# Two transformer layers on one core: W1 and W3 copied once into a layout by units, one load per unit, and a new order of the work

## The chip, the cores and the metric

One Trainium2 chip, of which the kernel uses one core. The metric is the time of one execution on the device in microseconds (us); lower is better. The kernel before took 2657.01 us in the median of three runs (2655.47 to 2658.84).

## What is computed

The input x has 2048 rows of 576 numbers (bf16). Two layers follow one another, with the same weights; each is an attention with a recurrent memory and then a gated feed-forward network (FFN). Cut to what matters:

```
def _A_ref(x, mem0, Wq, Wk, Wv, Wo, seg_len):      # 32 heads of 128, 8 memory rows, seg_len 32
    mem = mem0
    for s in range(n_seg):                          # 64 segments, one after the other
        h = concatenate([mem, x[:, s*32:(s+1)*32]]) # 40 rows
        q, k, v = h Wq, h Wk, h Wv
        p = softmax(where(mask, q k^T * 128**-0.5, -1e9))
        o = (p v) Wo
        mem = o[:, :8]                              # the next segment needs it
        outs.append(o[:, 8:])
def _B_ref(x, w1, w3, w2):                          # w1, w3: 576 x 4608, w2: 4608 x 576
    return (silu(x w1) * (x w3)) w2
for _ in range(2):
    x = x + _A_ref(layernorm(x), ...)
    x = x + _B_ref(layernorm(x), ...)
```

## The kernel before

**Steps.** The 64 segments of a layer form a chain through mem. The second layer runs eight segments (LAG) behind the first, so there are 72 steps; step t works on segment t of layer 0 and on segment t - 8 of layer 1. Steps 8 to 63 have both ("both", 80 columns per matmul), the first and the last eight have one layer (40 columns). After every four steps a job of FFN work becomes possible (128 rows of each layer).

**Pieces.** `make_nodes` (from line 248) cuts the work into nodes: an engine, a duration in us that the planner books, what they need, a priority, and the buffers they take and give back. On TensorE each kind has a letter (line 90): Q and q are the projections to q and k (512 rows of the contraction, and the last 64 rows as "tail"), S the scores, T a transpose of the softmax weights on TensorE (steps with one layer only), P the weighted sum, O and o the output projection and its tail, V, v, X, x, G, g the projections to v, F and f a unit of x w1 and x w3, W and w the products with w2 of two units, n, a, b the transposes behind a layernorm, p that of the attention's output, m that of mem0.

**Order.** `plan` (line 94) lays the nodes out in time. TensorE's sequence is written out by hand, as three strings of letters (lines 217 to 238): `ORDER = FIRST + FOUR * 11 + LAST`; FOUR is four steps. The other engines take, in the planner's time, the node that can start first. Evictions may go to ACT or DVE ("AD"). What the planner then emits is a fixed order per engine; the hardware waits on semaphores where a piece isn't ready.

**Modes.** TensorE can be used as a whole, in two column halves, or in row halves or finer. A node names its modes ("full/col"). The planner keeps the mode as long as the next node allows it, and books `SWITCHES` (line 38, 0.092 to 0.098 us) for a change.

**FFN weights.** A unit is 256 columns of w1 and w3 (18 units, NPR). `load_w13` (line 761) brings a unit with four DMAs issued by SP, two of 256 KB and two of 32 KB, into one of two buffers of the tile W13; the trace names them `W<-in_B_w_dram`. A row of a unit is 512 bytes in DRAM. `load_w2` brings 256 rows of w2 (288 KB, `W2C<-in_B_w_dram`). Both are read again for each of the 17 jobs that load them; the last job takes most of its weights from W and WV (`tail_load`), whose attention weights are dead by then.

**SP's queue.** SP issues, in one order: the attention weights, the unit loads, the loads of x for the layernorm (XN), and in steps with both layers the transposes of the softmax weights as DMAs (`ptr_dma`, line 1103, `PTS<-PB`). PTS has one buffer, so a transpose can only be issued when P has read the one before. POOL issues the loads of x for the residual (XR) and the stores, and clears PB after each transpose.

**Other tiles.** OT (four slots of 640 columns) takes the evicted results of P for O; YO holds the odd half of the last output tail until the memory columns and YTS are written; YTS collects a layer's outputs for p.

Every instruction is recorded by a helper: L659 are the matmuls, L662 ACT, L665 DVE, L668 SP's DMAs, L671 ACT's DMAs, L674 POOL's DMAs.

Of the kernel before, what the change touches and what calls it, by code (L numbers as in the profile page):

```python
# [13 lines left out]
P = 128  # L14
# [19 lines left out]
PTR = 112  # L34

# [6 lines left out]
POOLS = {"bank": 8, "qkt": 4, "sme": 2, "pb": 2, "pts": 1, "ot": 4,  # L42
         "xr": 3, "xn": 2, "w13": 2, "w2": 2, "htt": 4}
# [26 lines left out]
class Node:  # L70
    __slots__ = ("eng", "dur", "fn", "deps", "prio", "mode", "acq", "rel", "name", "lat", "outs", "left", "ready",
                 "start", "end", "by", "inst")

    def __init__(self, eng, dur, fn, deps=(), prio=0.0, mode=None, acq=(), rel=(), name="", lat=None):
        self.eng, self.dur, self.fn, self.prio, self.mode = eng, dur, fn, prio, mode.split("/") if mode else mode
        self.deps = [d for d in deps if d is not None]
# [13 lines left out]
KINDS = {"m0tr": "m", "L0tr": "a", "L1tr": "b", "POST": "p", "Ftr": "n", "QK": "Q", "QKt": "q", "SC": "S", "TR": "T", "PV": "P",  # L90
# [3 lines left out]
def plan(nodes, pools, letters):  # L94
# [17 lines left out]
    order = []  # L112

# [23 lines left out]
    while len(order) < len(nodes):  # L137
# [34 lines left out]
        t_eng[e] = n.end  # L172
        for s in n.acq:
# [38 lines left out]
def ewh(*ns):  # L212
# [5 lines left out]
    "maQqSQQvqqVSxXTqSPQSTOPXoTPOTPoOoOoQqqQvSSqVqQSQTPSTOPOToPToxPOOooQqqQSqvSaVQQSqTPSTPOOoTPoTPOOooQqqQSQSvqVQTSqX"  # L218
    "SPTPOTOPoToxPOOooQqqpQvSSVqnQfFSTFfqQPWSTOPFTOfPFTofoPOOooWQFfqqfFSQQSqqfFvVfTFSPQWTSFPXffOTFPOTOPWOooooaxQqqQSW"
    "FSQvfqTVfSFPQFTfqOPSWTOPFOTffoooPFOoWQqqvSQQSFfqVfSTWqFQFSPTfPOTWPoTOPOOooobQpvVqqqQQSnQqfxFSXqqfFQQQPSWFqqfQOfS"  # L220
# [6 lines left out]
    "QqqqqQppQQvVSSnnQFfqqQFqSfQQPFfqOwPoSWFffOPFWOowoPFOoFffqqQQQQqqWSwFSGgfqqQQQPQqqgWSSGFPFffggGGPwOFOPOOffooowoFv"  # L227
    "VqqqQQQWSFqfqqQQQSwWFPSFfqqfQQPwOSWFFPoffOOWPwOoooFfqqQQWaSqqQQQbSQqgqGSQPQqqgGSOPoGggOPGwOPooOo"
# [4 lines left out]
    "QPFSTOPofFTOPwTWPOOoooFfqfqQQSQSFvqfVfqFTQPSWwSTFPxXffTFPOOTWOPwOFooooFqffqQQSWwVvqfSQFfqTQPSWTwPOSFOTfFPwTOPWOo"  # L233
    "oooFqfqfFQQWSfqSFwvVQQTSqffPWwSTFFPOoTOWPoTwPOOoobQpqxqvVSnQXqfFSQTQSPFfqOoTSFfPTwPOOoofTFPFOowQfqqQSQSFvqfVTqfF"
    "PQTSwPSXffFTOOPwTOPFOooooFxqfQQqqSvVSQTQSFPfqfOTSPwoOTFPFTOPoofOowQQfqqFSSvVqQQSqTwPTSPOOFTofPTPOOooopfffFFFnwfw"
    "FFffFFwfFffFwffwFFFFffwFwfffFFFwffFFwfffFFww"
# [11 lines left out]
def make_nodes(em, nseg, pools, o=Opt, dma_bw=230e3, load_bw=345e3):  # L248
# [24 lines left out]
    def load(name, nbytes, prio, fn, deps=()):  # L273
        return node("DMA", nbytes / load_bw, fn, deps=deps, prio=prio, name=name, lat=2.0)

    ld_m0 = node("ACT", 0.1, em.load_m0(), prio=-90, name="m0", lat=2.5)
    ld_t = [load("ldt", kb(3 * R64, 4096), -10.0, em.load_tails(0)), node("ACT", 0.1, em.load_tails(1), prio=-120, name="ldt", lat=6.0)]
    node("ACT", 0.1, em.load_tails(2), prio=-80, name="ldt", lat=6.0)
# [3 lines left out]

    b = banks(1)
# [10 lines left out]
    def ln_nodes(tag, src, xn, deps, prio, writes, warm=False):  # L294
# [5 lines left out]
        d = node("PE", 5 * 0.056, em.ln_tr(xn, b, warm), deps=[c], prio=prio, mode="col", acq=[b], rel=[xn], name=tag + "tr")  # L300
# [24 lines left out]
    vx_ev, last_v, pvs = {}, [], {}  # L325

    def v_nodes(name, t, k, prio, tail_at, emit, strips, deps, tail_deps, free):
# [3 lines left out]
        m_ = node("PE", 8 * 0.2158 + 0.11, emit(b, False), deps=deps, prio=prio, mode=modes[0], acq=b, name=name)  # L331
        n = node("PE", 0.2158, emit(b, True), deps=deps + tail_deps, prio=prio + tail_at, mode=modes[1], acq=b, name=name + "t")
# [39 lines left out]
    def step(t):  # L372
# [6 lines left out]
        mm80 = max(c80 / 2.4 + 2.5, 25.0) / 1000  # L379
        rd = reads_ht.setdefault(t, [])  # L380

# [9 lines left out]
        for g, (h0, nh) in enumerate(GROUPS):  # L391
            qs, qe = [], []
            for uh, un in units(g, nl):
# [3 lines left out]
                m_ = node("PE", 8 * un * mm80, em.qk(t, uh, un, b), deps=hx + hm[:1] + ([ld_h[g]] if t == 0 else []),  # L397
                          prio=pq, mode="full", acq=[q] + b, name="QK")
                n = node("PE", un * mm80, em.qk_tail(t, uh, un, b), deps=hx + hm + ([ld_h[g]] if t == 0 else []), prio=pq + o.qkt, mode="row",
# [3 lines left out]
                for r in (0, 1):  # L403
                    cost = ew(un * 64, un * 16) if e == 0 else ew(un * 48, un * 32)
                    qe.append(node("AD", cost if nl == 2 else ew(un * 40), em.qk_ev(t, un, r, q, b[r]), deps=[m_, n], prio=t + o.ustep * uh / 4,
                                   rel=[b[r]], name="QKe"))
# [5 lines left out]
            sc = node("PE", nh * (0.0165 * nl if nl == 2 else 0.0255), em.scores(t, g, qs, s), deps=qe, prio=pf + o.sc, mode="col" if nl == 2 else "full/col",  # L412
# [5 lines left out]
            d = node("DVE", dve(w40) + 0.2, em.sm_sum(t, g, sme), deps=[c], prio=pf, name="sum")  # L418
            w = 0.168 * (4 - e if nl == 2 else 2) + nl * w40 / 960
# [18 lines left out]
            ot = Slot("ot")  # L438
# [998 lines left out]
```

## Time and profile before

| | us |
|---|---|
| median of three runs | 2657.01 |
| the profiled execution | 2657.81 |
| its span, first to last instruction | 2656.0 |
| TensorE (PE) busy in it | 2578.3 |
| DVE busy | 2004.1 |
| ACT busy | 1242.3 |
| POOL busy | 335.2 |

The granted TensorE clock is 0.992 of full speed in the mean. A busy PE is a PE with a matmul in flight; PEld are its weight loads, which run beside it. "idle before <-releaser" tells how long an engine stood idle before an instruction and whose end let it go; "issue" means that nothing in the profile explains the wait. The times of the timeline are us from the start of the span: start, length, engine, line, operation, result and operands, count.

### The profile page before, as it was taken

Reading aid. Unit: us, or ns where it says so; the run is one execution under the profiler, and the core shown is the slowest. Engines: PE = TensorE matmul, PEld = TensorE weight load, DVE = VectorE, ACT = ScalarE, POOL = GpSimd, SP = SyncE. Lnnn points to the kernel's source line nnn. Section 1 sums busy time; section 2 is a strip of 40 time slices with the busy share of each in tenths; the row PEclk is TensorE's granted clock in tenths of the full one; section 3 lists DMA queues with packets and bytes.
Section 4 is the critical chain, followed back from the end, with each engine's and each line's share of the span. In section 5 each row is a group of like instructions: output and inputs, shape, how many; then the busy total and the mean of one; then the engine's idle time right before and its main releaser. Section 6 shows DMA issues by size and latency. Waiting matters only on the chain.

```text
span 2656.0 us, 133410 instructions
## 1 busy us (share of the span) xinstructions
PE 2578.3 (97%) x59426; PEld 2216.6 (83%) x59426; DVE 2004.1 (75%) x5137; ACT 1242.3 (47%) x3495; POOL 335.2 (13%) x399
## 2 busy tenths in 40 slices
PE   6899999999999999999999999999999999999998
PEld 4788878888888888888888888888888888888887
DVE  4677777877787778778777877877787787777866
ACT  2555453444545444454544544454444445454443
POOL 1111111110101111010101101110110111011110
PEclk8899999999999999999999999999999999999999
DMA  9055746556554655555465555645565554554458
GB/s 322 4 153 150 182 101 152 128 131 157 117 141 108 152 135 126 155 128 139 109 143 134 138 146 125 146 106 151 122 147 139 132 140 106 129 139 131 130 155 244
DMA packets 690433, 371.48 MB, mean 140 GB/s; under 512 B 234328, under 2 KB 682592, under 8 KB 689216
## 3 DMA queue, kind: packets, MB, share of 16 engines
q1 hardware_dynamic: 686320, 355.08, 53.5%
q8 instruction: 464, 7.60, 1.2%
q0 software_dynamic: 3024, 6.93, 0.9%
q10 hardware_dynamic: 512, 0.94, 0.2%
q14 instruction: 113, 0.93, 0.1%
HBM read 306.72 MB, written 2.36 MB: 116 GB/s over the span
## 4 chain that ended last, share of the span: by engine, by line
PE 83%; DMA 9%; DVE 5%; ACT 1%; issue 1%; SPq 1%; POOL 0%; ACTq 0%; DVEq 0%; POOLq 0%
PE bank L659 83%; DMA PTS<-PB 5%; DMA W<-in_B_w_dram 1%; DMA W2C<-in_B_w_dram 1%; DVE STAT L665 1%; DMA WV<-in_A_Wv_dram 1%; DVE SME L665 1%; DVE PB L665 1%; SPq L668 1%; DVE V L665 0%; DMA W<-in_A_Wq_dram 0%; ACT V L662 0%; DVE XR L665 0%; DVE HTT L665 0%; DVE LNS L665 0%
## 5 line engine op out<-in xcount | busy, mean ns | idle before, releaser
L659 PEld LDWEIGHTS <-W 128*128 128x128 bf16 (+2 forms) x32464 | 1259.9, 100 | 118.1 <-issue 63.6
L659 PE MATMUL bank<-HT,W 128*128 128x80 bf16 (+3 forms) x23040 | 785.1, 197 | 16.1 <-issue 9.3
L659 PE MATMUL bank<-XTB,W 128*64 128x256 bf16 (+5 forms) x9424 | 658.9, 263 | 2.0 <-DMA W<-in_B_w_dram 2.0
L1093 POOL MEMSET PB<- 128x1024 bf16 x288 | 273.9, 951 | 1944.4 <-DMA PTS<-PB 1142.8
L662 ACT ACTIVATE QKT<-bank 128x256 bf16<-128x256 f32 (+4 forms) x1423 | 342.4, 320 | 246.4 <-PE bank L659 216.9
L659 PE MATMUL bank<-OT,WO 128*128 128x80 bf16 (+3 forms) x11520 | 421.2, 199 | 1.0 <-ACT OT L662 0.5
L662 ACT ACTIVATE V<-bank 64x512 bf16<-64x512 f32 (+1 forms) x605 | 339.6, 585 | 164.9 <-PE bank L659 158.4
L659 PEld LDWEIGHTS <-WO 128*128 128x128 bf16 (+1 forms) x11520 | 387.8, 102 | 34.0 <-issue 18.7
L659 PE MATMUL bank<-WV,HT 128*32 128x512 bf16 (+4 forms) x3768 | 370.4, 386 | 5.1 <-DMA WV<-in_A_Wv_dram 4.5
L659 PE MATMUL bank<-W2C,HTT 128*64 128x288 bf16 (+1 forms) x3216 | 321.8, 287 | 3.4 <-DMA W2C<-in_B_w_dram 2.8
L662 ACT ACTIVATE OT<-bank 128x320 bf16<-128x320 f32 x374 | 153.8, 437 | 313.2 <-PE bank L659 309.3
L665 DVE TENSOR_REDUCE STAT<-SME 104x8 f32<-104x320 f32 (+1 forms) x576 | 275.1, 478 | 27.9 <-ACT SME L662 22.3
L665 DVE TENSOR_TENSOR PB<-SME,STAT 40x128 bf16<-40x128 f32 (+4 forms) x912 | 275.4, 336 | 12.1 <-DVE STAT L665 0.4
L665 DVE SCALAR_TENSOR_TENSOR HTT<-HTT,bank 128x512 bf16<-128x512 bf16 (+1 forms) x324 | 201.5, 622 | 106.7 <-ACT HTT L662 103.7
L659 PEld LDWEIGHTS <-HT 128*32 128x32 bf16 (+4 forms) x3768 | 155.4, 100 | 145.2 <-issue 39.1
L659 PEld LDWEIGHTS <-HTT 128*64 128x64 bf16 (+1 forms) x3288 | 230.1, 105 | 40.8 <-issue 7.3
L662 ACT ACTIVATE HTT<-bank 128x512 bf16<-128x512 f32 (+1 forms) x324 | 173.9, 548 | 179.9 <-PE bank L659 178.3
L665 DVE SCALAR_TENSOR_TENSOR XR<-bank,XR 128x288 f32<-128x288 f32 x574 | 241.5, 447 | 14.4 <-PE bank L659 11.0
L662 ACT ACTIVATE SME<-SME 104x320 f32<-104x320 f32 (+1 forms) x288 | 135.1, 469 | 241.4 <-DVE SME L665 238.1
L665 DVE TENSOR_TENSOR HTT<-HTT,bank 128x512 bf16<-128x512 bf16 (+1 forms) x324 | 203.7, 629 | 33.0 <-PE bank L659 0.5
L665 DVE CAST QKT<-bank 128x192 bf16<-128x192 f32 (+2 forms) x497 | 141.4, 328 | 104.7 <-PE bank L659 102.5
L665 DVE CAST V<-bank 64x512 bf16<-64x512 f32 (+1 forms) x259 | 177.3, 684 | 36.9 <-PE bank L659 33.0
(60 smaller groups left out, 1394.4 us busy)
## 6 DMA issues: line engine op xcount, KB each, us to landing
W<-in_B_w_dram SPq DMA_DIRECT2D x608, 256.0 KB, 3.9
W2C<-in_B_w_dram SPq DMA_DIRECT2D x304, 288.0 KB, 3.5
W<-in_B_w_dram SPq DMA_DIRECT2D x608, 32.0 KB, 3.9
W<-in_B_w_dram SPq DMA_DIRECT2D x16, 512.0 KB, 8.3
WO<-in_A_Wo_dram SPq DMA_DIRECT2D x4, 1152.0 KB, 10.0
XR<-in_A_x_dram POOLq DMA_DIRECT2D x16, 288.0 KB, 4.0
WV<-in_B_w_dram SPq DMA_DIRECT2D x8, 576.0 KB, 7.3
W<-in_A_Wq_dram SPq DMA_DIRECT2D x16, 256.0 KB, 5.8
```

Of the source, the lines that this page charges most:

```text
L659: self.ch("PE", self.nc.tensor.matmul(out, lhsT=lhsT, rhs=rhs, start=start, stop=stop, skip_group_check=True, **k))
L662: self.ch("ACT", self.nc.scalar.activation(*a, **k))
L665: self.ch("DVE", getattr(self.nc.vector, fn_)(*a, **k))
L668: self.ch("SP", self.nc.sync.dma_start(out=out, in_=in_))
L1093: return lambda n: self.ch("POOL", self.nc.gpsimd.memset(self.T.PB[:, pb.i, 0:GROUPS[g][1]], 0.0))
```

## The change

1. Behind the last load of WO, SP issues three copies of ten DMAs each from W1 and W3 to new DRAM tiles XW0 to XW2 (six units each), laid out so that a unit's nine blocks for one partition lie behind one another (4608 bytes).
2. `load_w13` becomes one DMA per unit from there. The planner makes a unit's load wait for its copy.
3. The planner books SP's issue time and the time in the DMA rings apart (`ring`), with new durations for several nodes.
4. The loads of x for the layernorm of groups 1 and 2 are issued by POOL, not SP.
5. OT gets eight slots of 320 columns; YO is gone, its 64 rows go to the last OT slot of the step; YTS shrinks from ten to nine blocks.
6. The strings FIRST, FOUR and LAST are written anew, with the same letters in the same numbers (709, 208 and 604).

The diff also brings code that works ahead on q and k (`PRE`, `ahead`, `xq`); PRE is empty, so none of it runs.

```diff
-POOLS = {"bank": 8, "qkt": 4, "sme": 2, "pb": 2, "pts": 1, "ot": 4,
-         "xr": 3, "xn": 2, "w13": 2, "w2": 2, "htt": 4}
+POOLS = {"bank": 8, "qkt": 4, "sme": 2, "pb": 2, "pts": 1, "ot": 8,
+         "xr": 3, "xn": 2, "w13": 2, "w2": 2, "htt": 4, "stage": 8}
...
+        if e == "DMA":
+            ring = max(ring + n.ring, n.end + n.lat)
+            n.lat = ring - n.end
...
 FOUR = (
-    "QqqqqQppQQvVSSnnQFfqqQFqSfQQPFfqOwPoSWFffOPFWOowoPFOoFffqqQQQQqqWSwFSGgfqqQQQPQqqgWSSGFPFffggGGPwOFOPOOffooowoFv"
-    "VqqqQQQWSFqfqqQQQSwWFPSFfqqfQQPwOSWFFPoffOOWPwOoooFfqqQQWaSqqQQQbSQqgqGSQPQqqgGSOPoGggOPGwOPooOo"
+    "QqqqqQppQQvVSSnnQFQfqqFQfqqfFPQSwWFPSffOOFPWFOPwOooooFfqfqQQQwQqqSWFSGfqqgQQwPQfgqqQSGSFPFWfggGGPOwOWPOOooooFffq"
+    "qQQQSFVvqqQQQqfqwFSaWFSPFfqqfQQOPSwWFffPFOOPWOwooooFfqqqQQWQSqqQQQSbQgqqqGSQPgGSOPGggOPGwOPoooOo"
 )
...
+    copied = [[node("DMA", 5.5, em.copy_w13(i), deps=ld_o[-1:], prio=-1.0 + 0.1 * i, lat=2.5, ring=CPX, name="W13c")] for i in range(COPIES)]
...
-                tr = node("DMA", 1.27 * nh / 8, em.ptr_dma(t, g, pb, pts), deps=[pbs], prio=pf - 0.02, acq=[pts], name="TR", lat=2.45)
+                tr = node("DMA", 1.25 * nh / 8, em.ptr_dma(t, g, pb, pts), deps=[pbs], prio=pf - 0.02, acq=[pts], name="TR", lat=TRLAT, ring=TRX)
...
-                        ld = [node("DMA", kb(1152, 256) / dma_bw, em.load_w13(pr_, w13), prio=prio - 1, acq=[w13], lat=2.8, name="W13")]
+                        ld = [node("DMA", 0.5, em.load_w13(pr_, w13), deps=after + copied[pr_ * COPIES // NPR], prio=prio - 1, acq=[w13], lat=2.2, ring=W13X, name="W13")]
...
-        ld = node("DMA" if g else "ACT", 0.8 if g else 0.1, em.load_xn(g, xn), deps=reads_ht.get(4 * g - 3, [])[:1], prio=4 * g - 3.0 if g else -100, acq=[xn],
-                  name="ldxn", lat=2.5)
+        ld = node(("SWD" if g < 3 else "DMA") if g else "ACT", 0.6 if g else 0.1, em.load_xn(g, xn), deps=reads_ht.get(4 * g - 3, [])[:1], prio=4 * g - 3.0 if g else -100, acq=[xn],
+                  name="ldxn", lat=(3.9 if g < 3 else 2.5) if g else 9.6, ring=XNX if g > 2 else 0.0)
...
+    def copy_w13(self, i):
+
+        def f(n):
+            k = NPR // COPIES
+            fs = slice(i * k * 2 * P, (i + 1) * k * 2 * P)
+            for kind, wd in ((0, self.a.w1), (1, self.a.w3)):
+                for c in range(4):
+                    self.dma(self.T.XW[i][:, :, 4 * kind + c, :].rearrange("u p f -> p u f"), wd[c * P:(c + 1) * P, fs].rearrange("p (u f) -> p u f", u=k))
+                self.dma(self.T.XW[i][:, kind * R64:(kind + 1) * R64, 8, :].rearrange("u p f -> p u f"), wd[4 * P:D, fs].rearrange("p (u f) -> p u f", u=k))
+        return f
+
     def load_w13(self, pr, w13):
-        def f(n):
-            fa = pr * 2 * P
-            W = self.T.W13[:, w13.i]
-            for kind, wd in ((0, self.a.w1), (1, self.a.w3)):
-                self.dma(W[:, 4 * kind:4 * kind + 4], wd[0:4 * P, fa:fa + 2 * P].rearrange("(c p) f -> p c f", p=P))
-            for kind, wd in ((0, self.a.w1), (1, self.a.w3)):
-                self.dma(W[kind * R64:(kind + 1) * R64, 8], wd[4 * P:D, fa:fa + 2 * P])
-        return f
+
+        k = NPR // COPIES
+        return lambda n: self.dma(self.T.W13[:, w13.i], self.T.XW[pr // k][pr % k])
```

More of the change, by code (lines that the diff above doesn't have):

```diff
@@ L34 @@
 PTR = 112
+PRE = ()
+TRLAT = 2.0
+TRX, W13X, W2X, XNX, CPX = 0.95, 1.55, 0.95, 0.5, 17.7
+COPIES = 3
+AHEAD = True
+BACK = 4
+GATES = {1: "WO1", **{i: "WO3" for i in range(2, 8)}}
 TIED = True
@@ L963, in qcols, with ahead, qk_rhs @@
         return (q0, q0 + SW) if self.both(t) else (q0 + 16 - 8 * role(t), q0 + 56 - 8 * role(t))
+    def ahead(self, t):
+        return t // 4 in PRE and self.both(t)
+    def qk_rhs(self, t, rows, c):
+        q0, q1 = self.qcols(t)
+        H_ = self.ht(t)
+        if not self.ahead(t):
+            return H_[rows, c, q0:q1], q1 - q0
+        if role(t):
+            return H_[rows, c, q0 + 32:q0 + 80], 48
+        x = H_[rows, c, q0 + 56:q0 + 80]
+        return bass.AP(x.tensor, x.offset, [list(v) for v in x.ap][:1] + [[-56, 2], [1, 24]]), 48
@@ L971, in f @@
         def f(n):
-            q0, q1 = self.qcols(t)
-            w = q1 - q0
-            HTt = self.ht(t)
             first = self.begin(b)
-            for c in range(4 if first and t == 0 else 0):
+            for c in range(4 if first and t == 0 and not PRE else 0):
                 for _ in range(3):
```

243 lines of the change are left out of this document (170 added, 73 removed).

## The prediction

> **What bounds the kernel now.** I read the page first, then busy time and idle time by stage (the windows), then TensorE's waits, whole and by stage, then single places in the timeline.
>
> ```profile
> span 2656.0 us, 133410 instructions
> PE 2578.3 (97%) x59426; PEld 2216.6 (83%) x59426; DVE 2004.1 (75%) x5137; ACT 1242.3 (47%) x3495; POOL 335.2 (13%) x399
> ```
>
> TensorE works 97% of the span; the next engine, DVE, 75%. The change removes no matmul, so it can only win what TensorE idles or spends between matmuls: 2656.0 - 2578.3 = 77.7 us idle. Where that lies, the windows tell (columns: window, length, busy us of PE, PEld, DVE, ACT, POOL, then granted clock, DMA share, GB/s):
>
> ```profile
> 0.00:66.00 66.00, 42.91 (x955) 28.71 (x955) 27.42 (x64) 15.86 (x35) 10.16 (x22) 0.90 0.96 324
> 66.00:140.00 74.00, 65.17 (x2085) 55.72 (x2077) 53.44 (x139) 41.73 (x96) 12.74 (x14) 0.86 0.02 4
> 140.00:400.00 260.00, 248.38 (x6573) 212.32 (x6569) 200.03 (x541) 131.09 (x371) 36.41 (x43) 0.99 0.62 150
> 400.00:2250.00 1850.00, 1832.46 (x40376) 1586.72 (x40373) 1421.45 (x3638) 872.01 (x2550) 226.33 (x265) 1.00 0.56 134
> 2250.00:2656.00 406.00, 389.41 (x9456) 333.09 (x9453) 301.78 (x758) 181.64 (x445) 49.55 (x56) 0.99 0.56 154
> ```
>
> Idle: 23.1, 8.8, 11.6, 17.5 and 16.6 us. The first 66 us are paced by the weights (DMA share 0.96); then the DMA engines have nothing to do until 140 us (0.02). In the long middle TensorE misses 17.5 of 1850 us and the DMA engines are 0.56 busy, so no transfer bounds it on average. What ends the waits:
>
> ```profile
> PE bank L659 <- DMA PTS<-PB: 14.9, 25, 1.1
> PE bank L659 <- issue: 12.3, 14, 2.0
> ...
> PE bank L659 <- ACT PTS L662: 8.0, 12, 2.0
> ...
> PE bank L659 <- DMA W2C<-in_B_w_dram: 2.8, 7, 0.6
> ...
> PE bank L659 <- DMA W<-in_B_w_dram: 2.0, 3, 1.0
> ...
> PE bank L659 <- DMA PTS<-PB: 12.4, 19, 1.1
> ```
>
> (The last row is that of 400 to 2250 us alone; the second number is how often, the third the longest.) The loads that the change rebuilds cost TensorE 2.0 us (W, that is W1 and W3) and 2.8 us (W2C). The softmax transposes, which share SP's queue with them, cost 14.9 us, 12.4 of them in the middle.
>
> **The change part by part.**
>
> *Copies.* W1 and W3 are 2 x 576 x 4608 x 2 bytes = 10.6 MB, read and written once, in 30 issues on SP behind the WO loads. Rows of SP's and TensorE's timelines, of the windows and of the table of DMA issues (KB each, us to landing):
>
> ```profile
> 39.46 7.73 SPq L668 DMA_DIRECT2D WO<-in_A_Wo_dram  x4
> ...
> 59.01 0.47 SPq L668 DMA_DIRECT2D XN<-in_A_x_dram  x1
> 140.88 4.54 SPq L668 DMA_DIRECT2D W<-in_B_w_dram  x8
> ...
> 139.79 1.28 PE L659 MATMUL bank<-XTB,W 64*128 64x128 bf16 x20
> ...
> 1840.50:1843.30 2.80, 2.80 (x83) 2.80 (x80) 1.08 (x2) 0.91 (x2) 0.95 (x1) 1.00 1.04 327
> 30.00:40.00 10.00, 5.51 (x131) 2.81 (x126) 0.99 (x3) 1.29 (x3) 0.00 (x0) 0.79 1.01 405
> ...
> W<-in_B_w_dram SPq DMA_DIRECT2D x608, 256.0 KB, 3.9
> out_dram<-XN SPq DMA_DIRECT2D x2, 72.0 KB, 1.6
> ```
>
> WO is issued by 47.2 us; the first FFN matmul runs at 139.8. A unit's load lands 3.9 us after its issue, so the copies have to end by 136 us, 89 after 47; SP has nothing else between, since the XN load at 59.01 (and two more) moves to POOL, where an x load takes 0.6 us of a 13% engine. A copy inside DRAM is not in this trace. From the rows: 512-byte rows of W1/W3 come in at 327 GB/s (1840.5 to 1843.3), wider rows of the start at 405. At 405 the copy takes 26 us, at 327 33 us; if each byte counts twice, 65 us; by the only store whose landing stands alone (72 KB in 1.6 us, 46 GB/s, mostly latency) 231 us. I take 65, nearest to the row with the same 512-byte pieces: done at 112 us, 24 us of cover left, cost 0. Late it becomes when 10.6 MB take over 89 us, below 119 GB/s. All three copies count, as the first load is queued behind all of them. The first load's wait holds up on SP only the other unit loads, W2C loads and later transposes (the first transpose is issued at 251 us).
>
> The Trainium skill, "DMA: Bandwidth & Descriptors", section "Latency and other measured facts", gives copies between DRAM tensors at 207 to 214 GB/s, and 103 at unlucky row pitches; an estimate by that page is 50 us, or 103 us and then 14 us late. No run here shows it yet.
>
> While the copies run, TensorE is in short matmuls and fetches its instructions fast. Its "issue" waits of 140 to 400 us (short matmuls, DMA share 0.62) and of 0 to 140:
>
> ```profile
> PE bank L659 <- issue: 4.0, 5, 1.4
> ...
> PE bank L659 <- issue: 0.3, 1, 0.3
> ```
>
> The second row has the first 66 us in it, at share 0.96. So I book +1 us (0 to +5).
>
> *Unit loads.* Four issues become one, 304 times; the 256-column rows of 512 bytes become 4608 bytes per partition. Rows of the views by tile (ns least, median, most), of SP's timeline, of the chain of waits (1794.80) and of TensorE's timeline:
>
> ```profile
> L668 SPq DMA_DIRECT2D W<-in_B_w_dram x1248: 367/508/2917, 47.2 to 2641.9; - x179
> L668 SPq DMA_DIRECT2D W2C<-in_B_w_dram x304: 367/416/1907, 53.9 to 2604.9; - x152
> ...
> DMA to landing us min/median/max: 2.9/3.1/5.6
> 1790.37 1.98 SPq L668 DMA_DIRECT2D W2C<-in_B_w_dram  x2
> 1792.39 2.22 SPq L668 DMA_DIRECT2D W<-in_B_w_dram  x4
> 1794.80 5.58 DMA PTS<-PB
> ...
> 1137.86 6.23 SPq L1103 DMA_TRANSPOSE PTS<-PB  x2
> 1142.34 0.45 PE L659 MATMUL bank<-PTS,V 128*128 128x80 bf16 x8 [0.78 <-DMA PTS<-PB]
> ...
> 2066.24 0.45 PE L659 MATMUL bank<-PTS,V 128*128 128x80 bf16 x8 [0.59 <-DMA PTS<-PB]
> ```
>
> SP spent 4 x 0.508 = 2.0 us on a unit; one issue like W2C's takes 0.4 to 0.5, so 1.5 us x 304 = 460 us of SP's time go. In the rings a unit's 590 KB take 1.80 us at 327 GB/s and 1.46 at 405: 0.35 us x 304 = 106 us, all of it beside TensorE. What TensorE can get back is what it waits behind these loads: 2.8 + 2.0, less 1.0 in the final stage, whose loads do not change: bounds 0 to -3.8, I take -2. And the transposes: issue to landing (the row of min, median and max is theirs) is 2.9 us at least, 3.1 in the median, but 5.58 at 1794.80, right behind a unit load and two W2C loads. The wait at 1142.34, though, has no load near it: it ends a landing of 4.4 us, from 1137.86 on, with only transposes on SP. The same place waits in 3 of 9 periods, the last time at 2066.24. So the loads cause part of the 14.9 us. Bounds: -14.9, and +29 (first rival); I take -3, nearer to no change, because the new order also places weighted sums closer (below).
>
> The Trainium skill, same page, section "Specifications", speaks against this part: transfers from 512 bytes up run at line rate, so the old rows would be as good as the new. The rows agree within 19% (327 against 405 GB/s). By the page the rings save nothing, and only the terms -2 and -3 would shrink, by less than 5 us together.
>
> *Order.* TensorE's sequence has the same 3601 pieces. The planner keeps a mode (full, column halves, row halves) as long as the next piece allows it. Counted so off the two order strings, the switches fall from 286 to 284 in FIRST, from 66 to 60 in FOUR, which is played 11 times, from 208 to 204 in LAST: 1220 to 1148, 72 fewer. The price of one:
>
> ```profile
> 1004.82 1.32 PE L659 MATMUL bank<-HT,W 128*128 128x80 bf16 x32
> 1005.98 2.24 PE L659 MATMUL bank<-XTB,W 128*128 128x256 bf16 x20
> ...
> 1011.43 0.32 PE L659 MATMUL bank<-HT,W 64*128 64x80 bf16 x8
> 1011.68 0.43 PE L659 MATMUL bank<-QKT 128*64 128x40 bf16 x16
> ```
>
> 32 matmuls of 80 columns take 1.16 us start to start, 36 ns each. The eight half-row ones run in pairs, 4 x 36 = 0.145 us, but 0.25 pass until the column mode starts: 0.105 us for the switch. 72 x 0.10 = -7.2 us, and nothing can hide it on an engine that is busy 99% there. This is my firmest term (-6.5 to -7.6).
>
> In the first 140 us, transposes by TensorE (T) wait for ACT to bring PTS back. A T directly followed by its P stands 8 times in the old FIRST, 4 times in the new. "ACT PTS" is 8.0 us over 12 times, 0.67 each: four fewer give -2.7, I take -3, bounds -8 and +3, since the steps there are a chain (a step's memory columns need the step before) and a gap filled can open again.
>
> In FOUR the last P's move closer: "P o G g g O P" becomes "P G g g O P", one half-width output tail (0.15 us) and two switches less.
>
> ```profile
> 1445.44 0.45 PE L659 MATMUL bank<-PTS,V 128*128 128x80 bf16 x8
> ...
> 1449.51 0.45 PE L659 MATMUL bank<-PTS,V 128*128 128x80 bf16 x8
> ```
>
> Here P follows P in 4.07 us without a wait; the new distance is 3.7 to 3.8. PTS has one buffer, so between two P lie the P itself, 0.5, and the landing, 3.1 in the median: 3.6. It just fits.
>
> *At no cost:* OT in eight half-width slots instead of four (same bytes), YO moved into such a slot, YTS packed to nine blocks: as many evictions and transposes as before, on ACT and DVE, which idle 53% and 25%.
>
> **Sum.** Switches -7.2, early T/P -3, transposes -3, load waits -2, issue +1 early and -2 later (lighter rings; 0 to -4): -16.2. The profiled execution took 2657.81 us (span 2656.0 and 1.8 around it): 2641.6. It stood 0.8 above the median of the runs, 2657.01, so 2641 us.
>
> **The rivals.**
>
> 1. *The landing is the bound at the close P's.* With the pieces of the strings laid end to end at such durations, six of FOUR's sixteen P's start within 4.6 us of the last, against three before. Where the landing takes 4.4 us instead of 3.1, as at 1142.34, each costs 0.8 us; in a third of the periods, as there, or in all. For: one PTS buffer. Against: lighter rings. Three more places x 12 periods x 0.8 x 1/3 = +10, and the -3 lost: 2654. If the landing is 4.4 us in every period: +29, 2673, slower; it turns from gain to loss where the landing passes 4.0 us in every period.
> 2. *The copies are late.* At a quarter of the 512-byte load rate, 82 GB/s, 10.6 MB take 130 us, end at 176, and the first FFN waits 40 us: 2681. It decides below 119 GB/s, and outweighs the gain below 100. For: only the poor store row. Against: one-way rates of 327 to 405.
> 3. *All waits on DMA go, issue waits too:* -7.2 - 14.9 - 3.8 - 9 (issue) - 4 (early) = -39: 2618.
> 4. *The clock.* It was granted at 0.88 up to 140 us, a loss of 0.10 x 66 + 0.14 x 74 = 17 us, in the stretches where TensorE idles most; fuller stretches there could return half of it: 2632.
> 5. *The loads are not faster at all* (the 19% above do not appear): 2646, inside the first case.
>
> **How the numbers follow.** Forecast 0.48 (own range 2630 to 2650); rival 1 in a third of the periods 0.17, in all 0.07; copies late 0.08; all waits gone 0.12; clock 0.08. A measurement of this kernel tells about 0.2%, 5.3 us, from no change. Faster: 0.48 + 0.12 + 0.08 = 0.68; same 0.17; slower 0.07 + 0.08 = 0.15. The range 2616 to 2662 leaves out the slower cases and a little below.
>
> **What would show it.** Copies: their landing before 136 us, no TensorE wait on W near 140. Loads: about 0.5 us of SP per unit. Switches and waits: a period of FOUR near 152.9; it was 153.9, nine of them lying between these two:
>
> ```profile
> 687.86 3.24 PE L659 MATMUL bank<-HT,W 128*128 128x80 bf16 x96 [0.34 <-ACT HT L662]
> ...
> 2073.14 3.24 PE L659 MATMUL bank<-HT,W 128*128 128x80 bf16 x96 [0.34 <-ACT HT L662]
> ```
>
>  Transposes: the wait on PTS at 12 us or less; above 20, rival 1. Wrong would be the forecast if idle in 400 to 2250 us rose above 17.5 us, or if a wait of over 5 us stood before the first FFN matmul.

## The result, and the profile after

The kernel after took 2732.72 us in the median of four runs (2730.29 to 2738.61), beside 2656.24 for the kernel before on the same chip: 1.0291 times as long, interval 1.027 to 1.0313. The change costs 76 us; I had forecast a gain of 16.

The page of the kernel after, its first lines, and the windows at the same places as for before (window, length, busy us of PE, PEld, DVE, ACT, POOL, granted clock, DMA share, GB/s):

```profile
span 2728.5 us, 131093 instructions
PE 2584.4 (95%) x59030; PEld 2222.7 (81%) x59030; DVE 2049.5 (75%) x5197; ACT 1223.1 (45%) x3435; POOL 336.4 (12%) x401
```

```profile
0.00:66.00 66.00, 39.12 (x884) 27.01 (x885) 27.38 (x64) 14.51 (x32) 9.40 (x21) 0.90 1.01 340
66.00:140.00 74.00, 60.30 (x1895) 51.61 (x1892) 48.14 (x125) 36.92 (x87) 13.18 (x15) 0.83 0.46 133
140.00:400.00 260.00, 252.23 (x6731) 215.35 (x6729) 206.86 (x558) 133.45 (x375) 37.32 (x44) 1.00 0.54 149
400.00:2250.00 1850.00, 1777.56 (x38529) 1539.34 (x38526) 1410.93 (x3550) 824.40 (x2405) 217.16 (x253) 1.00 0.51 130
2250.00:2728.00 478.00, 455.18 (x11013) 389.34 (x11009) 356.17 (x904) 213.82 (x537) 59.35 (x69) 0.99 0.51 145
```

TensorE's work is the same (2584.4 us busy, before 2578.3); its idle time grew from 77.7 to 144.1. The long middle is where it lies: 1850.0 - 1777.56 = 72.4 us idle, before 17.5. The DMA engines are not fuller there: 0.51 busy, before 0.56. So something waits for single transfers, not for bandwidth. TensorE's waits over the whole span (us, times, longest):

```profile
PE bank L713 <- DMA PTS<-PB: 58.1, 50, 3.3
PE bank L713 <- issue: 20.2, 24, 2.4
PE bank L713 <- DMA W<-XW: 11.4, 18, 1.6
...
PE bank L713 <- ACT PTS L716: 4.4, 7, 1.2
```

And from 400 to 2250 us alone:

```profile
PE bank L713 <- DMA PTS<-PB: 54.4, 46, 3.3
PE bank L713 <- DMA W<-XW: 10.9, 17, 1.6
```

The softmax transposes cost 58.1 us instead of 14.9, the unit loads 11.4 instead of 2.0. One such place, in SP's timeline:

```profile
723.32 0.34 SPq L722 DMA_DIRECT2D W<-XW  x1
723.76 1.61 SPq L1233 DMA_TRANSPOSE PTS<-PB  x1
```

In the chain of waits (start, us, what):

```profile
723.76 5.52 DMA PTS<-PB
```

And in TensorE's timeline:

```profile
729.32 0.45 PE L713 MATMUL bank<-PTS,V 128*128 128x80 bf16 x8 [1.70 <-DMA PTS<-PB]
```

A unit load is issued 0.44 us ahead of a transpose. The transpose lands 5.52 us after its issue (the least is 2.9), and the weighted sum P stands for 1.70 us. Steps (from 0) counted off by the 320 matmuls of q and k in each, the stages of the profiled executions compare so (us; the kernels e1 to e16 follow below; "costs" are the durations that the planner books):

| kernel | letters | costs | unit loads | first 16 steps | next 48 | last 8 |
|---|---|---|---|---|---|---|
| before | old | old | four each | 532.6 | 1848.3 | 275.1 |
| after | new | new | one each | 533.4 | 1915.0 | 280.1 |
| e1 | old | old | one each | 543.4 | 1840.5 | 273.8 |
| e8 (e1, two x loads on POOL) | old | old | one each | 538.1 | 1842.2 | 273.6 |
| e13 (after's instructions) | old | old | one each | 540.7 | 1842.4 | 273.2 |
| e3 | old | new | one each | 539.4 | 1870.3 | 276.0 |
| e15 | new | old | one each | 541.5 | 1903.7 | 284.7 |
| e4 | new | old | four each | 531.2 | 1925.4 | 276.7 |
| e9 | old | old | none | 520.4 | 1840.6 | 263.5 |
| e5 | new | new | none | 524.9 | 1834.5 | 269.7 |
| e10 | FOUR loosened | new | one each | 535.4 | 1894.7 | 276.1 |
| e14 | old | old | one each, late copies | 545.8 | 1843.9 | 273.7 |
| e16 | FIRST new, rest old | old | one each | 536.0 | 1842.5 | 269.1 |

The two profiled spans differ by 72.5 us; 67 of them lie in the middle 48 steps, 44 of which play FOUR (the last four belong to LAST).

### The profile page after: what moved, and what is told of

Same layout as the page of the kernel before. It is cut to its first block, busy times and chain, and to the rows that moved or that the text cites. A ratio compares the mean times of both kernels' runs of the same rounds, so it can differ in the third digit from the quotient of the medians.

```text
span 2728.5 us, 131093 instructions
## 1 busy us (share of the span) xinstructions
PE 2584.4 (95%) x59030; PEld 2222.7 (81%) x59030; DVE 2049.5 (75%) x5197; ACT 1223.1 (45%) x3435; POOL 336.4 (12%) x401
## 4 chain that ended last, share of the span: by engine, by line
PE 70%; DMA 16%; DVE 9%; issue 2%; ACT 1%; SPq 1%; POOL 0%; ACTq 0%; DVEq 0%; POOLq 0%
PE bank L713 70%; DMA PTS<-PB 9%; DMA W<-XW 3%; DVE STAT L719 2%; DMA XN<-in_A_x_dram 2%; DVE XR L719 1%; DVE PB L719 1%; DVE SME L719 1%; DVE HTT L719 1%; DMA W<-in_B_w_dram 1%; SPq L722 1%; DMA WV<-in_A_Wv_dram 1%; DVE V L719 1%; DVE LNS L719 1%; ACT V L716 0%
## 5 line engine op out<-in xcount | busy, mean ns | idle before, releaser
L713 PE MATMUL bank<-HT,W 128*128 128x80 bf16 (+3 forms) x23040 | 794.8, 197 | 23.8 <-issue 11.8
L713 PE MATMUL bank<-XTB,W 128*64 128x256 bf16 (+5 forms) x9312 | 667.8, 263 | 16.8 <-DMA W<-XW 11.4
L716 ACT ACTIVATE QKT<-bank 128x64 bf16<-128x64 f32 (+4 forms) x1413 | 339.4, 318 | 319.9 <-PE bank L713 303.6
L713 PE MATMUL bank<-OT,WO 128*128 128x80 bf16 (+3 forms) x11520 | 405.9, 198 | 4.9 <-issue 4.4
L716 ACT ACTIVATE V<-bank 32x512 bf16<-32x512 f32 (+1 forms) x583 | 330.7, 585 | 125.9 <-PE bank L713 119.5
L713 PE MATMUL bank<-WV,HT 128*32 128x512 bf16 (+5 forms) x3680 | 369.3, 384 | 6.0 <-DMA WV<-in_A_Wv_dram 4.2
L716 ACT ACTIVATE OT<-bank 128x320 bf16<-128x320 f32 (+2 forms) x416 | 159.9, 401 | 292.9 <-PE bank L713 285.1
L713 PEld LDWEIGHTS <-HT 128*32 128x32 bf16 (+5 forms) x3680 | 152.7, 99 | 147.5 <-issue 39.1
L719 DVE SCALAR_TENSOR_TENSOR HTT<-HTT,bank 128x512 bf16<-128x512 bf16 (+1 forms) x324 | 200.7, 619 | 75.4 <-ACT HTT L716 72.5
L719 DVE CAST V<-bank 64x512 bf16<-64x512 f32 (+1 forms) x281 | 192.4, 685 | 26.3 <-PE bank L713 21.5
L719 DVE CAST QKT<-bank 128x64 bf16<-128x64 f32 (+2 forms) x507 | 145.9, 331 | 83.2 <-PE bank L713 79.1
```

The source lines that it names most:

```text
L713: self.ch("PE", self.nc.tensor.matmul(out, lhsT=lhsT, rhs=rhs, start=start, stop=stop, skip_group_check=True, **k))
L716: self.ch("ACT", self.nc.scalar.activation(*a, **k))
L719: self.ch("DVE", getattr(self.nc.vector, fn_)(*a, **k))
```

## The experiments

**Theory 1:** the new FOUR leaves some P's too little work ahead of them (behind their scores S, or behind the P before, which frees PTS) for a transpose that shares the DMA engines with a unit load. **Rivals:** the single loads themselves; the copies; the planner's new costs, which divide the evictions anew; SP's queue.

### One part at a time (e1 to e4)

e1 puts copies and single loads into before; e2 takes both out of after; e3 puts the old strings into after; e4 the new strings into before.

```diff
-                        ld = [node("DMA", kb(1152, 256) / dma_bw, em.load_w13(pr_, w13), prio=prio - 1, acq=[w13], lat=2.8, name="W13")]
+                        ld = [node("DMA", kb(1152, 256) / dma_bw, em.load_w13(pr_, w13), deps=copied[pr_ * COPIES // NPR], prio=prio - 1, acq=[w13], lat=2.8, name="W13")]
```

> The kernel before with its order, bookings and tiles, but W1 and W3 copied once and each unit loaded as one transfer. Theory 'order' (the new strings and bookings leave the softmax transposes too little room): about as before, 2640 to 2665 us, PTS waits near 15 us. Theory 'loads' (a whole unit in one transfer directly ahead of a transpose makes it land 2 us later): most of the loss is here, above 2710 us, PTS waits above 45 us. Both together needed: 2665 to 2710.

> The changed kernel with its order and bookings, but without the copies, each unit again loaded by four transfers from W1 and W3. Theory 'order': still slow, above 2715 us. Theory 'loads': 2640 to 2665 us, PTS waits below 20 us, landing of the transposes back at 3.1 us in the median.

> The changed kernel, loads and bookings included, with the old three strings for TensorE. If the strings are what costs: 2640 to 2665 us. If the bookings cost (they set the order of loads and transposes on SP and who evicts): above 2700 us, PTS waits above 40 us. Theory 'loads': above 2710 us too; e1 tells these two apart.

> The kernel before, loads and bookings included, with the new three strings. If the strings alone cost: above 2700 us. If not: the 72 fewer switches show, 2645 to 2655 us.

Measured: e1 2660.9 us, ratio 1.0024 (1.0012 to 1.0035); e2 2743.32, 1.0334 (1.0307 to 1.0361); e3 2689.59, 1.0136 (1.011 to 1.0162); e4 2742.8, 1.0334 (1.0309 to 1.0358). So the loads aren't the loss: with the old order they change little, with the new one they save some 10 us (2743.3 to 2732.7), which the intervals barely tell apart. The strings alone cost 87 us in before's frame. But e3, between its two expectations, is still 29 us above e1 with the same letters and loads: there is a second loss in after. The waits from 400 to 2250 us in e1:

```profile
PE bank L662 <- DMA PTS<-PB: 7.3, 11, 1.1
...
PE bank L662 <- DMA W<-XW: 0.2, 1, 0.2
```

e4 has old loads and nearly the same waits there:

```profile
PE bank L659 <- DMA PTS<-PB: 48.2, 45, 3.0
PE bank L659 <- DMA W<-in_B_w_dram: 9.0, 14, 1.4
```

SP's timeline shows one of them in another place:

```profile
722.17 4.84 SPq L668 DMA_DIRECT2D W<-in_B_w_dram  x8
727.17 1.26 SPq L1103 DMA_TRANSPOSE PTS<-PB  x1
```

The transpose comes to its turn on SP only after eight issues of 4.84 us. Here, with four issues per load, the time is lost in SP's queue; with one, in the place above, it was lost in the transfer (5.52 us). The cost moved; it did not go.

### What P waits for (e5, e9, e6, e7, e10, e11)

e5 is after, e9 before, both without the unit loads after the first two:

```diff
+            if w13.i in self.held:
+                return
+            self.held.add(w13.i)
```

> The changed kernel with every unit load after the first into each of the two buffers left out (302 of 304), so that it computes most FFN units with stale weights; W2C loads, copies, order and bookings stay. If the close P's wait because the transposes land late behind unit loads: PTS waits fall from 58 us to under 20, landing to 3.1 us in the median, time 2670 to 2695 us. If the new strings stand too close for a transpose with free rings as well: PTS waits above 40 us, above 2705 us.

> The kernel before without its unit loads after the first two, one for each buffer (the FFN then multiplies with those weights again and again, so its numbers aren't the reference's; every matmul stays). It asks what the old order pays for the unit loads; the new order paid 99 us (2732.7 against 2633.7 without them). Theory 1 (the new strings leave too little work between S and P for a transposition that lands behind a unit load; the old ones leave enough): the old order pays little, 8 to 20 us, so 2636 to 2648, and stays behind the new order without loads, which has fewer changes of mode. Rival (unit loads slow every order alike, through shared engines or the port): it pays 50 us or more, 2605 or less.

e5 took 2633.69 us, ratio 0.9917 (0.9902 to 0.9932), e9 2627.0, 0.989 (0.9875 to 0.9905). The long middle of e5 in the windows:

```profile
400.00:2250.00 1850.00, 1837.11 (x40315) 1602.36 (x40313) 1471.14 (x3708) 861.89 (x2519) 227.61 (x266) 1.00 0.29 66
```

Its wait on PTS there:

```profile
PE bank L714 <- DMA PTS<-PB: 8.7, 10, 1.7
```

And the landing of its transposes, in the view of PTS:

```profile
DMA to landing us min/median/max: 2.9/2.9/5.2
```

Without loads the wait on PTS in the middle falls from 54.4 to 8.7 us, and the median landing is the least one. The new order pays 99 us for the unit loads, the old one 30, and in the 48 steps the difference is plain: new 1915.0 - 1834.5 = 80.5, old with single loads 1840.5 - 1840.6, nothing. So the wait needs both, the new order and the unit loads, as theory 1 says. Both kernels are faster than expected (2670 to 2695 and 2636 to 2648). The old order's 30 us are more than the 8 to 20 expected: 8 in the 48 steps, with four loads a unit, and 12 each in the first and the last steps. And e9 doesn't stay behind e5 in all, as I had expected, only in the 48 steps.

Where the unit loads fall, the traces of 400 to 2250 us tell. In after 54 of 185 transposes are issued within 1 us behind a unit load; where the trace tells the landing, they land after 4.92 us in the mean, those with no unit load in the 6 us before them after 3.05. With the old letters and single loads (e1, e3, e13, e16) not one of the 191 to 194 stands so close.

e6 lets ACT's queue issue the unit loads; e7 lets the planner hold a load back when a transpose is due within 2 us:

```diff
-        return lambda n: self.dma(self.T.W13[:, w13.i], self.T.XW[pr // k][pr % k])
+        return lambda n: self.adma(self.T.W13[:, w13.i], self.T.XW[pr // k][pr % k])
```

> The changed kernel with the unit loads issued by ACT instead of SP, so that they are in another queue than the transposes on the same 16 engines. If the late landing is the queue's order (a transpose behind 576 KB in one ring): landing about 3.3 us in the median and 4.5 at the ninth decile, PTS waits under 30 us, 2690 to 2715 us, unless ACT loses as much by waiting for buffers. If the engines themselves are the limit: landing stays at 3.5 or more, 2725 to 2745 us.

> The changed kernel, except that the planner holds a load on SP back when a transpose becomes ready within 2 us by its bookings. If loads slipped in ahead of transposes are the cause: PTS waits 20 to 40 us, 2695 to 2720 us, W waits up from 11 to some 20. If not: 2725 to 2740 us.

e6: 2770.43 us, 1.0433 (1.0416 to 1.045). e7: 2748.55, 1.0338 (1.0309 to 1.0367). Waits from 400 to 2250 us in e6:

```profile
PE bank L713 <- DMA PTS<-PB: 52.6, 49, 4.1
```

And in e7:

```profile
PE bank L718 <- DMA W<-XW: 37.5, 25, 2.7
PE bank L718 <- DMA PTS<-PB: 22.4, 19, 2.7
```

Both times lie above all that was expected. With the loads in another queue TensorE waits as long for PTS (52.6 against 54.4). The 32 transposes of this stretch that are issued within 1 us behind a load land after 5.12 us in the mean (in after 4.92), so another queue doesn't keep the load out of a transpose's way. But late landing isn't all of e6's wait: at the third and fourth P of a period the transpose starts 1.6 to 1.7 us behind the P before, when its softmax is done; and the median landing, 3.3 us, was to speak for the queue's order. In e7, served first, the transposes make TensorE wait less (22.4), and now the loads are late (37.5): the wait changes its name. (e7's trace is that of its fastest execution, 2730.43 us.)

e10 is after with a FOUR whose letters are moved by a few places until each P stands further behind its S where a load falls between; it has 85 changes of mode a period instead of 60.

```diff
-    "QqqqqQppQQvVSSnnQFQfqqFQfqqfFPQSwWFPSffOOFPWFOPwOooooFfqfqQQQwQqqSWFSGfqqgQQwPQfgqqQSGSFPFWfggGGPOwOWPOOooooFffq"
+    "QqqqpQpqQQvVnSSnQqfqFQfqQqFSFPfQwWFSPfOOfoowPFWFOPOooFffqqQQQwSqqQWFSgfGqqQQwPQqqQgfSGSFPFWfggGGPOwOWPOOofoooFqq"
...
```

> After with another FOUR and nothing else changed: the same letters, moved by a few places until each P stands further behind its S wherever a unit load is due between them. It pays for this with 25 more changes of mode per period (85, after 60, before 66), worth 2.6 us a period by 0.105 us each. Theory 1 (P's too close for the landing behind a unit load): waits on PTS within 400 to 2330 us fall from 55.9 to under 25 us, the period falls from 159.6 to 156 or 157 us in spite of the changes of mode, total 2680 to 2705. Rival A (bookings of evictions or the many small waits make the loss, not the distance S to P): the period rises by the changes of mode, to 162, total 2755 to 2770. Rival B (the transpositions land later whatever the order, as with loads from another queue): PTS waits stay above 40 us, total at or above 2733.

2710.96 us, 1.0211 (1.0195 to 1.0226). Its waits from 400 to 2250 us:

```profile
PE bank L713 <- DMA PTS<-PB: 10.7, 17, 1.4
PE bank L713 <- DVE QKT L719: 6.6, 9, 1.1
PE bank L713 <- issue: 6.2, 35, 0.7
PE bank L713 <- DVE SME L719: 4.2, 8, 0.7
PE bank L713 <- ACT OT L716: 4.2, 11, 0.4
...
PE bank L713 <- DMA W<-XW: 1.7, 3, 0.9
```

The waits on PTS and W fall from 65.3 to 12.4 us, and the kernel is 22 us faster in spite of 25 more changes of mode a period. Rivals A and B are out. It missed the 2680 to 2705 expected; the QKT, SME, OT and issue waits, 21.2 us, are this string's own. How it helps, the trace tells more exactly than I had put it: the second to fourth P of a period start 5.6, 4.4 and 5.6 us behind the end of the P before (in after 5.5, 6.1 and 4.8, its waits included), but their transposes land in 3.3 to 3.9 us instead of 4.3 to 5.0, since the unit loads now fall elsewhere: 11 of 187 transposes are issued within 1 us behind one.

e11 tells after's planner the landings that the trace shows; the letters stay.

```diff
-TRLAT = 2.0
+TRLAT = 2.6
...
-acq=[w13], lat=2.2, ring=W13X, name="W13")]
+acq=[w13], lat=4.4, ring=W13X, name="W13")]
```

> After with its letters, and the planner told what the trace shows: 4.4 us for the landing of a unit load behind its issue (it had 2.2) and 2.6 for that of a transposition (it had 2.0). Only the bookings can change by this: which of VectorE and ScalarE evicts what, and the order in the DMA queue; the letters stay. Theory 1 (the loss is in the letters): no change beyond 12 us either way, 2720 to 2745, PTS waits still above 45 us in all. Rival (the loss is in bookings made with landings that are too short): it falls by 25 us or more, to 2707 or less.

2763.88 us, 1.0403 (1.0385 to 1.0421): neither expectation. The wait on PTS from 400 to 2250 us fell to 36.7, but one on DVE for HTT came up, 31.5. Bookings do move time, and with these letters they couldn't repair it.

### The second loss: the planner's costs (e12, e13, e15)

e12 gives e3 two of before's costs, e13 all of them; e15 gives all of them to after with the new letters. Two of the lines:

```diff
-            w = (1.04 - 0.07 * e + 0.3 * (pre and e) if nl == 2 else 0.46) * nh / 8
+            w = 0.168 * (4 - e if nl == 2 else 2) + nl * w40 / 960
...
-acq=[pts], name="TR", lat=TRLAT, ring=TRX)
+acq=[pts], name="TR", lat=2.45)
```

> The kernel of old strings in after's frame (2689.6 us), with before's costs for two steps of the plan: PB's normalisation on VectorE (1.34 us for a group where after's plan says 1.04) and the V matmuls. VectorE then gets 710 evictions where it got 759, in the plan with the old order and the new loads 695. Theory (29 us between the two kernels with the old strings are evictions that the new costs move to VectorE, which then are late for PE): most of it comes back, 2662 to 2675, waits of PE on what VectorE writes at half or less. Rival (something else of the frame: OT's slots, the order of the DMA queue): it stays at 2683 to 2695.

> The kernel of old strings in after's frame (2689.6 us; 2684.5 with two of before's costs) with all of before's costs in the plan, so that its evictions are divided nearly as in the old order with the new loads (691 on VectorE, there 695, with after's costs 759). After's instructions stay: OT in single slots, the odd rows of Y in OT, YTS packed, the loads of XN 1 and 2 from GpSimd's queue. Theory (the plan's costs make the 29 us): 2653 to 2666, the middle stage (16 to 64 of the 72 steps) back at 1839 to 1845 us. Rival (the changed instructions make it): 2676 to 2690, PE's waits on XR and QKT stay at 10 us or more.

> After with all of before's costs in the plan; letters, loads, copies and instructions stay after's. Theory (the letters leave P's too close to S, the costs are a second loss that shows with any letters): the close P's stay, so at least half of the loss stays; 2695 to 2745, waits on PTS above 40 us. Rival (the new letters are sound and only the costs were wrong): 2650 to 2670, as with the old letters.

e12: 2684.48 us, 1.0106 (1.0091 to 1.0121). e13: 2655.72, 1.0002 (0.9989 to 1.0015). e15: 2725.75, 1.0251 (1.0233 to 1.027). The window from 400 to 2250 us in e3:

```profile
400.00:2250.00 1850.00, 1820.95 (x39866) 1570.42 (x39890) 1449.32 (x3624) 834.09 (x2483) 222.22 (x259) 1.00 0.51 133
```

Waits that e3 has there and e1 has not:

```profile
PE bank L713 <- DVE XR L719: 6.7, 11, 0.6
...
PE bank L713 <- ACT OT L716: 2.6, 11, 0.2
...
PE bank L713 <- DVE V L719: 1.8, 9, 0.2
```

The same window in e13:

```profile
400.00:2250.00 1850.00, 1834.02 (x40479) 1589.21 (x40475) 1427.62 (x3646) 874.56 (x2559) 225.53 (x264) 1.00 0.51 134
```

With the new costs DVE is busy 1449 us in this window and ACT 834; with the old ones 1428 and 875. Evictions went from ACT to DVE, and PE waits for XR and V, which DVE writes, and for OT. With all old costs the 34 us are gone: the costs make this loss, and the instructions of after, which e13 keeps, are innocent. That the moved evictions are how they make it isn't shown. In e12 DVE's busy time is nearly back, and still it is only 5 us faster than e3, in the range of its rival:

```profile
400.00:2250.00 1850.00, 1819.26 (x39869) 1568.38 (x39894) 1430.97 (x3611) 848.35 (x2495) 221.47 (x260) 1.00 0.51 133
```

So how busy DVE is in the mean doesn't make the loss; which of the other costs makes the rest wasn't tried. With the new letters the costs weigh only 7 us (2732.7 against 2725.8). The letters weigh 70 with the old costs (2725.8 against 2655.7) and 43 with the new ones (2732.7 against 2689.6). So the letters are the main cause; the two losses don't simply add.

### The copies, and a faster kernel (e8, e14, e16)

e8 is e1 with the loads of XN groups 1 and 2 on POOL; e14 is e1 with the copies issued one by one, from 59.6 to 346.4 us, between the unit loads of the first two FFN passes, which take their units from W1 and W3 with four transfers; e16 is e13 with the new FIRST.

```diff
+                    if j < 2 and pieces:
+                        i, kind, c = pieces.pop(0)
+                        copied[i].append(node("DMA", 1.8, em.copy_w13(i, kind, c), deps=[ff], prio=prio, lat=2.5, name="W13c"))
```

> The old order and bookings with copies and single loads, and the x loads of groups 1 and 2 moved from SP's queue (behind the copies) to POOL. The old order with new loads took 2660.9 us with 6.7 us of wait on one x load. If that wait is what the copies cost early: 2650 to 2655 us, below the kernel before. If the copies cost by starving instruction fetch: 'issue' waits stay near 18 us and the time at 2656 to 2661.

> The old order with the new loads (2660.9 us), with the thirty copies taken from the stretch behind the attention weights and issued one by one, each behind a unit of the first two FFN passes (130 to 380 us); those two passes load their units from W1 and W3 with four transfers each, as before does. Theory (the copies cost 7 to 10 us because they run beside the short matmuls in front of the first FFN, and cost little beside the long ones): the fourth step begins at 130 us again (141 with early copies), the middle stage keeps 1840 us, total 2644 to 2652, 0.2 to 0.5% faster than before. Rival (the copies' work costs the same wherever it stands, since it delays loads and transpositions): the 7 to 10 us turn up between 130 and 380 us, total 2654 to 2662.

> The kernel with old letters and before's costs in after's frame (2655.7 us), with the new FIRST in place of the old; FOUR and LAST stay old. After's own FIRST reaches the sixteenth step at 533.4 us, the old one in this frame at 540.7. Theory (the new FIRST gives what was predicted for it: looser T and P, two changes of mode less, and so makes up for the copies): the sixteenth step at 532 to 536 us, the rest as before it, total 2647 to 2652. Rival (the 7 us come from the new costs and not from the letters): the sixteenth step at 539 us or later, total 2654 to 2658.

e8: 2654.78 us, 1.0004 (0.9992 to 1.0016), in the theory's range but not below before. It reaches step 16 5.3 us earlier than e1, which had 6.7 us of wait on that x load; its waits for issue are 18.4 us, as the rival had them. e14: 2665.44, 1.0037 (1.0022 to 1.0051). Its step 4 begins at 128.5 us (e1: 140.8, before: 130.3), but steps 8 to 11 take 150.4 us (e1: 137.5), and step 16 begins later than in e1. From 130 to 546 us TensorE waits 7.9 us for PTS and 3.3 for an x load (before: 3.3 and nothing). So the rival's account holds, though the time lies above its range: the copies cost in both places. e16: 2648.22, 0.9965 (0.9952 to 0.9978), as its theory said, and the one kernel with all its loads that beats before. Its long middle in the windows:

```profile
400.00:2250.00 1850.00, 1837.83 (x40545) 1593.12 (x40543) 1431.85 (x3656) 876.18 (x2559) 226.55 (x265) 1.00 0.52 135
```

Two of its waits there:

```profile
PE bank L713 <- DMA PTS<-PB: 6.2, 10, 1.1
...
PE bank L713 <- DMA W<-XW: 0.5, 1, 0.5
```

And two matmuls in TensorE's timeline, nine periods apart:

```profile
689.66 3.24 PE L713 MATMUL bank<-HT,W 128*128 128x80 bf16 x96 [0.34 <-ACT HT L716]
...
2071.26 3.24 PE L713 MATMUL bank<-HT,W 128*128 128x80 bf16 x96 [0.34 <-ACT HT L716]
```

Its middle has 12.2 us idle and a period of (2071.26 - 689.66) / 9 = 153.5 us, 0.4 below before's. The profiled spans of e13 and e16 differ by 8.7 us (the medians by 7.5): 4.7 lie in the first 16 steps, which FIRST orders; some 4 are in the last eight, whose letters are the same, and aren't explained.

## Why the prediction was wrong, point by point

**The bound** was read rightly: TensorE, with nothing to win but its idle time and its switches. Where I failed was in what could be lost there.

**Copies.** In time, as forecast: issued by 92.6 us, landing 6.6 us behind their issue, and TensorE has no wait on a unit load before the first FFN matmul. SP's timeline, and the page's table of DMA issues:

```profile
51.72 40.91 SPq L722 DMA_DIRECT2D XW<-in_B_w_dram  x30
```

```profile
XW<-in_B_w_dram SPq DMA_DIRECT2D x24, 384.0 KB, 6.6
```

10.6 MB in about 47.5 us are 223 GB/s; the 65 us that I took were too careful. The Trainium skill's 207 to 214 GB/s ("DMA: Bandwidth & Descriptors", "Latency and other measured facts") was the better estimate. Their cost was not the 1 us (0 to 5) that I booked: with the old letters and costs e13 reaches step 16 8.1 us after before, e8 5.5. Part of it is seen from 66 to 140 us, where e13 ran 1988 matmuls in 62.0 us and before 2085 in 65.2, and in its waits for issue there:

```profile
66.00:140.00 74.00, 62.02 (x1988) 52.81 (x1989) 48.24 (x125) 37.86 (x88) 11.95 (x13) 0.88 0.45 130
PE bank L713 <- issue: 4.5, 5, 1.9
```

After has 6.3 us of such waits in this stretch, e8 5.7; before, e9 (no copies) and e14 (copies elsewhere) have none. What the engine lacks there, the profile doesn't say.

**Unit loads.** The forecast was -2 for waits, -3 for transposes, -2 for lighter rings. With the old letters that is what came in sum: 1848.3 to 1840.5 us in the 48 steps of e1, -7.8; and e9, which has no unit loads at all, is no faster there. Only 3.2 of the 7.8 us are idle time; the rest lies in time that counts as busy. The loads are lighter, as forecast: from 400 to 2250 us the DMA engines are 0.56 busy at 134 GB/s in before, 0.52 at 135 GB/s in e1, and 0.29 at 65 GB/s in e9. An estimate from these is 0.23 of their time for the unit loads instead of 0.27. SP's time for a unit, from the view of W, and the loads' landing, from the page:

```profile
L722 SPq DMA_DIRECT2D W<-XW x304: 319/339/2468, 92.7 to 2669.8; - x152
```

```profile
W<-XW SPq DMA_DIRECT2D x304, 576.0 KB, 4.2
```

0.34 us for a unit, where I said 0.5. The copies eat what this wins, so that loads and copies together come out even (e13, 1.0002).

**Switches.** -6.1 us between e5 and e9 in the 48 steps, where nothing waits for unit loads; my count for FOUR was 66 x 0.105 = 6.9. The two kernels differ in their costs too, so this is no clean measurement, but it agrees. In after nothing of it can be seen beside the waits.

**Early T and P.** -3 forecast. The 8.0 us of wait on ACT's PTS that I put into the first 140 us are those of the whole span; 6.3 lie there. With the new FIRST alone they fell there from 6.5 (e13) to 3.3 (e16), -3.2, and step 16 begins 4.7 us earlier. Right in place and in size.

**The step that failed: the term "transposes -3"**, and under it the sentence "PTS has one buffer, so between two P lie the P itself, 0.5, and the landing, 3.1 in the median: 3.6. It just fits." For the P's that it looked at, it held. I sorted the P's of after between 400 and 2250 us by their place among FOUR's sixteen. The last three, which start 3.4 to 3.7 us behind the end of the P before, wait 0.01 us in a period: no unit load is near, and their transposes land in 2.9 to 3.0 us. But the sentence used the median landing, and the sum asked nothing of the P's that start further apart. Six of these (the second to fifth, tenth and twelfth) wait 4.6 us a period, and their transposes land in 3.3 to 5.2 us in the mean. At the second, third, tenth and twelfth a unit load is mostly issued less than 1 us ahead of the transpose, at the fourth 1.5 us; the fifth has none near and waits only 0.2 us. At the second and fourth the transpose had waited for the P before, at the twelfth for its softmax, at the third and tenth for its turn on SP: what frees it differs, and a unit load just ahead is what the five share.

The work between the P's is mostly no less than in the old order: without the waits, the second to fourth P start 5.3, 4.9 and 4.0 us behind the end of the P before in after, and 4.6, 4.9 and 5.1 in e1. So theory 1 named the right transfers, but the new letters did their harm more by where the unit loads fall than by less work ahead of a P. I had seen a landing of 5.58 us right behind unit loads, and booked -3 because loads become lighter. But the one load that replaced four brings the same 576 KB, now 0.4 us ahead instead of 2. In the middle the wait on PTS went from 12.4 to 54.4 us, +42 where I had -3, and that on W, 2.0 in the whole span, to 11.4.

Two matmuls of after, nine periods apart, against the forecast of a period near 152.9:

```profile
695.01 3.24 PE L713 MATMUL bank<-HT,W 128*128 128x80 bf16 x96 [0.34 <-ACT HT L716]
...
2133.77 3.24 PE L713 MATMUL bank<-HT,W 128*128 128x80 bf16 x96 [0.34 <-ACT HT L716]
```

(2133.77 - 695.01) / 9 = 159.9 us.

**The second step that failed: "At no cost".** I priced the evictions by their number and by idle shares (ACT 53%, DVE 25%). The planner's new durations, which stood in the diff, got no term in the sum, without a reason. They cost 34 us with the old letters (e13 against e3) and 7 with the new (e15 against after).

**Rivals.** Rival 1 named the right resource, PTS and its landing, and its sign that decides (a wait on PTS above 20 us) came true; but it put the loss at the closest P's, at 0.8 us each, and so at 29 us at most. The idle time of 400 to 2250 us passed the 17.5 us named as the sign of a wrong forecast, with 72.4. Copies late, all waits gone and loads not faster did not happen. The clock went the other way (0.990 of full speed, before 0.992): no gain.

**What stays open.** The 48 steps lost 66.7 us, and idle time in them explains 59 (16.1 to 75.1); the other 8 are in time that counts as busy. Which of the planner's costs makes the most of the second loss, and by which wait, wasn't separated, nor all that the copies do to the steps beside them.

## What to carry to other kernels

A transfer that is short in the median is not short behind a big one: for each consumer ask what was issued just ahead of its transfer, and compare the work that covers it with that landing, not with the median. When an order and the costs that it was made with change together, try the old order with the new parts first (e1 alone shows that the loads are harmless with the old letters), and then each string by itself: the useful one (FIRST; e16 is 0.35% faster than before) was hidden behind the harmful one.

## What the hardware showed that I had not expected

- A transpose issued 0.4 us behind a 576 KB load landed in 5.52 us instead of 2.9; 54 transposes within 1 us behind such a load took 4.92 us in the mean. With the loads in ACT's queue it was 5.12 us (32 transposes): separate queues didn't separate the transfers.
- A copy of 10.6 MB within DRAM, pieces of 512 bytes to blocks of 4608, ran at about 223 GB/s, and the first 16 steps took 5 to 11 us longer with it beside short matmuls (e8, e13, e1), and 13 us longer with it between the unit loads (e14).
- Single unit loads, which raise the traffic from 65 (e9) to 135 GB/s (e1), cost nothing in the old order that can be seen in the 48 steps (1840.5 us with, 1840.6 without).
